# Sparse attention with a mixing network on one core: the last pair of heads of the first batch takes another way to its weights, its division and its low parts

## The chip, the cores and the metric

The kernel runs on one core of a Trainium2 chip (trn2). The metric is the time of one execution on the device in microseconds (us), the median of several executions. Lower is better. The engines are named as in the profile: PE is TensorE, DVE is VectorE, ACT is ScalarE, POOL is GpSimd, SP is SyncE, which here only issues DMAs.

## The reference, cut to what matters

There are 4 batches, 8 heads of width 64, and 576 tokens. Attention keeps the 32 largest scores of each row and gives them a softmax. Its output goes through two mixing networks.

```python
scores = scale * np.matmul(q, k.transpose(0, 1, 3, 2))          # [4, 8, 576, 576]
kth = np.partition(scores, -32, axis=-1)[..., -32:-31]
scores = np.where(scores >= kth, scores, -1e9)
attn = softmax(scores)                                           # sum + 1e-9 below the line
x = np.matmul(attn, v)                                           # then [batch, 576, 512]

theta = x @ w_theta                                              # network 1
y = einsum(w_tok_r, x * cos(theta)) + einsum(w_tok_i, x * sin(theta))
u = x + y
x = u + relu(u @ w_ch)

h = relu(x @ w_in)                                               # network 2
u, v = h[..., :512], h[..., 512:]
out = (u * (w_spatial @ layernorm(v) + b_spatial)) @ w_out
```

All of it is float32. PE multiplies rounded halves: each operand is split into a high part and a low part, and one product is three matmuls (high by high, high by low, low by high; `mm3`, L576 to L578).

## The kernel before, in words

**Attention.** A visit is one pair of heads of one batch, 16 visits in all, 4 per batch. A visit has 9 tiles: tiles 0 to 7 hold 128 rows of one head, tile 8 the last 64 rows of both. Two tiles make a group (G = 2), so there are 144 tiles and 72 groups, 18 groups per batch. For each group these steps follow one another:

- `scores`: PE multiplies (L449), ACT copies the result to the tile `x` (L453).
- `topk`: DVE folds each row into winners and losers (L468, L469), takes the best 8 of the losers as a guard (L472), and finds the 32 largest in four rounds of MAX8 (L478) and MATCH_REPLACE8 (L481). The threshold is the last value of `mx`. Two small ACT operations (L489, L490) and one on DVE (L491) make the numbers of the tile `cf` from it.
- `weigh`: ACT computes the sign of x minus the threshold into `sg` (L500) and the exponential of `x` in place (L501). POOL multiplies the two (L89, four pieces a group, since the helper `Pieces` cuts every POOL operation to at most 300 columns). What is below the threshold comes out negative.
- `transpose`: PE turns the result (L511), ACT copies it with a Relu, which makes the negatives zero (L512).
- `values`: PE multiplies by v (L533), with a column of ones that gives the row sums; ACT copies the result to `xr`. `normalise` divides: two small DVE operations (L564, L565), then a multiplication on POOL into `xn` (L89). The last visit of the first batch (visit 3) is normalised in four parts, as its tiles come.

**The networks.** The class `Front` prepares network 1 of a batch when its attention is done: it transposes `xn` (L689), splits it into high (`zah`) and low parts (`zal`, `last`), multiplies by w_theta, and takes sines and cosines on ACT, for which ACT loads another table and then loads the one of the exponential again. `rotate` then makes the operands of the token mixing: `zah`, `zal` with the cosine and `zbh`, `zbl` with the sine. The function `middle` runs the rest: 72 token-mixing products per batch accumulate in `ps_m`, DVE adds each result to the tile F (`F<-ps_m,F`), and so on through both networks. `last` is the last product. While one batch is in the networks, the next one is in attention: PE has the products between the matmuls of attention, and DVE has the top-k.

**What sets the order.** The program writes groups of attention, and after each half group lets the network's generator (`advance`) run until a quota is used up. A scheduler then orders each engine's instructions by its own model of time and by priorities: attention's steps have `AHEAD`, the front of the first batch has `FRONT` (higher), operations by `upool`, `udve`, `uact` have `URGENT`. Each engine then works through its list in that order, and waits at the first instruction whose inputs are not there. Beside this runs `conv`, which splits the weights (L163 to L170 and L211, tiles `w_raw` and `w_f`) and stores the parts by DMA.

```python
self.turns = [upool, udve] if b == B - 1 else [upool, upool]                    # who makes low parts
pool.tensor_tensor(sg, x, sg, op=OP.mult)                                       # weigh
pool.tensor_tensor(xn[:, i], xr[:, i, :, 0:D], rs[:, i, :, None]..., op=OP.mult)  # normalise
```

Of the kernel before, what the change touches and what calls it, by code (L numbers as in the profile page):

```python
# [10 lines left out]
F32 = mybir.dt.float32  # L11
F32R = mybir.dt.float32r
I32 = mybir.dt.int32
AF = mybir.ActivationFunctionType
# [10 lines left out]
def sparse_attention_then_moe_kernel(  # L25
# [310 lines left out]
    def run(exact):  # L336
# [96 lines left out]
        X, SG, MX, PT = {}, {}, {}, {}  # L433
        PER = NP * NT

        def scores(n):
            i, b, j, t = tiles[n]
            qs, ks, kl, dg = heads[i]
            ps = psum.tile([128, 2, 512], F32, name="ps_s")
            for c in range(2):  # L440
                o = ps[:, c, 0:HALF]
                m = slice(c * HALF, (c + 1) * HALF)
                if t < 8:
                    i, s = divmod(t, 2)
                    terms = [(qs[s][:, i * 128:(i + 1) * 128], k) for k in (ks[s], kl[s])]
                else:
                    terms = [(dg[s], k) for s in range(2) for k in (ks[s], kl[s])]
                for a, (q, k) in enumerate(terms):
                    pe.matmul(o, q, k[:, m], start=a == 0, stop=a == len(terms) - 1)  # L449
            if n % G == 0:  # L450
                X[n // G] = att.tile([128, G, S], F32, name="x", bufs=3)
            x = X[n // G][:, n % G]
            act.activation(x.rearrange("p (c n) -> p c n", c=2), ps[:, :, 0:HALF], AF.Copy)  # L453

        def topk(g):

            x = X[g]
            mx = att.tile([128, G, 32], F32, name="mx")
            mm = att.tile([128, G, S], F32, name="mm", bufs=1)
            if exact:  # L460
                src, mr = ([t[:, i] for i in range(G)] for t in (x, mm))
            else:


                z = att.tile([128, G, QUARTER + 16], F32, name="z", bufs=1)
                for t, lo, mid, hi, win in ((x, 0, HALF, S, mm), (mm, 0, QUARTER, HALF, z)):
                    a, b = t[:, :, lo:mid], t[:, :, mid:hi]
                    dve.tensor_tensor(win[:, :, 0:mid], a, b, op=OP.max)  # L468
                    dve.tensor_tensor(mm[:, :, mid:hi], a, b, op=OP.min)  # L469
                for k, losers in enumerate((slice(LOSERS, S), slice(QUARTER, LOSERS))):  # L470
                    for i in range(G):
                        dve.max(out=z[:, i, QUARTER + 8 * k:QUARTER + 8 * k + 8], in_=mm[:, i, losers])  # L472
                src = [z[:, i] for i in range(G)]
                mr = [mm[:, i, 0:QUARTER + 16] for i in range(G)]
            for r in range(4):
                top = [mx[:, i, 8 * r:8 * r + 8] for i in range(G)]
                for i in range(G):
                    last = dve.max(out=top[i], in_=src[i])  # L478
                if r < 3:
                    for i in range(G):  # L480
                        dve.match_replace(out=mr[i], in_to_replace=top[i], in_values=src[i], imm_value=NEG)  # L481
                    src = mr
            kth = mx[:, :, 31]
            if not exact:
                dve.tensor_tensor(flags[:, g], z[:, :, QUARTER + 7::8], mx[:, :, 31:32].to_broadcast([128, G, 2]),
                                  op=OP.is_gt)

            cf = att.tile([128, G, 3], F32, name="cf", bufs=3)
            act.activation(cf[:, :, 0], mx[:, :, 0], AF.Copy, scale=-0.125)  # L489
            act.activation(cf[:, :, 1], kth, AF.Abs, scale=ULP)  # L490
            dve.scalar_tensor_tensor(cf[:, :, 2], cf[:, :, 1], 1e-37, kth, op0=OP.max, op1=OP.subtract)  # L491
            MX[g] = cf
            GATE[g] = last.ins

        def weigh(n):
            x, cf = X[n // G][:, n % G], MX[n // G][:, n % G]
            if n % G == 0:
                SG[n // G] = att.tile([128, G, S], F32, name="sg", bufs=2)
            sg = SG[n // G][:, n % G]
            act.activation(sg, x, AF.Sign, bias=cf[:, 2:3])  # L500
            act.activation(x, x, AF.Exp, bias=cf[:, 0:1], scale=0.125)  # L501
            pool.tensor_tensor(sg, x, sg, op=OP.mult)
# [55 lines left out]
        def normalise(b, j, lo, hi):  # L558
            if lo == 0:
# [3 lines left out]
            rs = tmp.tile([128, 5, 2], F32, name="rs")  # L563
            dve.tensor_scalar(rs[:, i], xr[:, i, :, D], 1e-9, None, op0=OP.add)  # L564
            dve.reciprocal(rs[:, i], rs[:, i])  # L565
            pool.tensor_tensor(xn[:, i], xr[:, i, :, 0:D], rs[:, i, :, None].to_broadcast([128, hi - lo, 2, D]),
                               op=OP.mult)
            if hi == 5:
                if j == NP - 1:
                    WHOLE.add(b)  # L570
                pool.tensor_tensor(xn[64:128, 4], xr[0:64, 4, :, 0:D],
                                   rs[0:64, 4, :, None].to_broadcast([64, 2, D]), op=OP.mult)


# [86 lines left out]
        class Front:  # L661


            def __init__(self, b):
# [3 lines left out]
                self.za = [z[:, 0:2048].rearrange("p (k d) -> p k d", k=4) for z in zpair("a")]  # L668
                self.zb = None
                self.xh, self.xl = (z.rearrange("p k (c n) -> p k c n", c=4) for z in self.za)  # L670
                self.turns = [upool, udve] if b == B - 1 else [upool, upool]

            def z(self, k, d):
                return tuple(z[:, k, d] for z in self.za) if k < 4 else tuple(z[:, k - 4, d] for z in self.zb)
# [425 lines left out]
```

## Time and profile before

| what | value |
|---|---|
| median of 3 runs | 979.75 us (978.85 to 980.02) |
| profiled execution, its own time | 980.12 us |
| its span in the profile | 978.2 us |
| PE busy | 852.8 us (87%) |
| DVE busy | 822.4 us (84%) |
| ACT busy | 636.1 us (65%) |
| POOL busy | 597.0 us (61%) |

The span is the stretch from the first to the last instruction that the profiler recorded. The time of the execution is 1.9 us longer. All stretches below are counted from the start of the span. Top-k group 17, the last of the first batch, ends near 214 us, the last top-k group of all near 796 us; after that only the networks are left.

### The profile page before, as it was taken

To read this page: it belongs to the slowest core of one execution; us is meant where nothing else is said; L and a number is where in the kernel's file an instruction comes from. 1 tells how busy PE (TensorE), PEld (TensorE's weight loads), DVE (VectorE), ACT (ScalarE), POOL (GpSimd) and SP (SyncE) were. 2 spreads that over 40 slices of the span, in tenths; PEclk is the share of its full clock that TensorE was granted. 3 is DMA by queue.
4 is the path that set the end of the run, shared out by engine and by line. 5 is a ranking of instruction groups with operands and counts; after the bars stand their busy time and mean duration, and the time that the engine had idled before them with its cause. 6 is when DMAs were issued, how large, how long until landed. Compare 5 with 4: busy or idle time off the path is not lost.

```text
span 978.2 us, 18058 instructions
## 1 busy us (share of the span) xinstructions
PE 852.8 (87%) x5802; PEld 784.8 (80%) x5802; DVE 822.4 (84%) x2698; ACT 636.1 (65%) x1315; POOL 597.0 (61%) x749
## 2 busy tenths in 40 slices
PE   3748576679679999999999999899989999999997
PEld 2636455567569889897999998788889998889987
DVE  6999999999998998999899998999998971463552
ACT  5566677679777668877966778677956764350121
POOL 1798767576884867686576656775675464330030
PEclk9975666779679999999999999999999999999999
DMA  7797666555825743645352745372623545451221
GB/s 219 212 296 234 209 221 176 167 148 157 273 93 173 252 141 116 194 161 140 117 164 54 250 144 162 143 204 101 170 116 91 214 180 192 170 187 48 103 86 53
DMA packets 79395, 159.78 MB, mean 163 GB/s; under 512 B 36143, under 2 KB 40239, under 8 KB 71866
## 3 DMA queue, kind: packets, MB, share of 16 engines
q1 hardware_dynamic: 79290, 158.53, 51.5%
q8 instruction: 48, 0.79, 0.3%
q14 instruction: 57, 0.47, 0.1%
HBM read 108.63 MB, written 23.32 MB: 135 GB/s over the span
## 4 chain that ended last, share of the span: by engine, by line
PE 43%; DVE 28%; ACT 9%; DMA 8%; POOL 7%; issue 4%; SPq 2%; POOLq 0%; ACTq 0%; DVEq 0%
PE ps_m L578 9%; PE ps_m L576 9%; PE ps_m L577 9%; PE ps_v L533 6%; DVE mm L469 4%; DVE mx L478 4%; DVE mm L481 4%; PE ps_s L449 4%; PE ps_t L511 3%; DVE z L472 3%; DVE mm L468 3%; POOL sg L89 2%; DMA q<-hi 2%; POOL zbl L89 2%; ACT sg L500 1%
## 5 line engine op out<-in xcount | busy, mean ns | idle before, releaser
L89 POOL TENSOR_TENSOR sg<-x,sg 128x288 f32<-128x288 f32 x288 | 238.4, 857 | 135.0 <-ACT x L501 85.0
L533 PE MATMUL ps_v<-vc,ptb 128*128 128x65 f32 (+1 forms) x1280 | 179.2, 278 | 4.4 <-ACT ptb L512 4.4
L511 PE MATMUL ps_t<-ident,sg 128*128 128x128 f32 x648 | 137.4, 307 | 50.4 <-POOL sg L89 35.1
L533 PEld LDWEIGHTS ps_v<-vc,ptb 128*128 128x128 f32 (+1 forms) x1280 | 170.4, 202 | 13.2 <-ACT ptb L512 6.8
L511 PEld LDWEIGHTS ps_t<-ident,sg 128*128 128x128 f32 x648 | 96.0, 168 | 65.4 <-POOL sg L89 47.2
L500 ACT ACTIVATE sg<-x,cf 128x576 f32<-128x576 f32 x144 | 103.9, 769 | 54.1 <-DVE cf L491 50.4
L478 DVE MAX8 mx<-mm 128x8 f32<-128x160 f32 x432 | 120.2, 318 | 0.0
L512 ACT ACTIVATE ptb<-ps_t 128x640 f32<-128x640 f32 (+1 forms) x144 | 92.5, 642 | 31.7 <-PE ps_t L511 30.1
L449 PE MATMUL ps_s<-k,q 128*128 128x288 f32 x256 | 90.5, 365 | 23.5 <-ACT x L453 14.1
L501 ACT ACTIVATE x<-x,cf 128x576 f32<-128x576 f32 x144 | 108.3, 767 | 0.0
L453 ACT ACTIVATE x<-ps_s 128x576 f32<-128x576 f32 x144 | 92.3, 641 | 18.7 <-PE ps_s L449 15.4
L576 PE MATMUL ps_m<-w_t,zah 128*128 128x288 f32 (+2 forms) x272 | 97.7, 359 | 5.7 <-POOL zah L592 2.8
L578 PE MATMUL ps_m<-w_t,zal 128*128 128x288 f32 (+2 forms) x272 | 96.9, 357 | 0.5 <-POOL zal L89 0.5
L577 PE MATMUL ps_m<-w_t,zah 128*128 128x288 f32 (+2 forms) x272 | 95.7, 352 | 0.0
L472 DVE MAX8 z<-mm 128x8 f32<-128x312 f32 (+1 forms) x288 | 89.5, 372 | 2.0
L576 PE MATMUL ps_m<-w_t,zbh 128*128 128x288 f32 x288 | 85.3, 301 | 3.9 <-DVE F L592 2.1
L578 PE MATMUL ps_m<-w_t,zbl 128*128 128x288 f32 x288 | 84.9, 303 | 3.1 <-POOL zbl L89 3.1
L481 DVE MATCH_REPLACE8 mm<-mx,mm 128x160 f32<-128x160 f32 x288 | 87.7, 314 | 0.0
L577 PE MATMUL ps_m<-w_t,zbh 128*128 128x288 f32 x288 | 85.3, 300 | 0.0
L449 PE MATMUL ps_s<-kl,q 128*128 128x288 f32 x256 | 81.5, 329 | 0.0
L449 PEld LDWEIGHTS ps_s<-k,q 128*128 128x128 f32 x256 | 56.3, 220 | 29.9 <-ACT x L453 20.8
L89 POOL TENSOR_TENSOR raw<-raw,hi 128x288 fp32r<-128x288 f32 x60 | 55.7, 947 | 37.4 <-ACT hi L393 22.6
(167 smaller groups left out, 2438.8 us busy)
## 6 DMA issues: line engine op xcount, KB each, us to landing
k<-hi SPq DMA_DIRECT2D x60, 144.0 KB, 2.5
kl<-raw SPq DMA_DIRECT2D x60, 144.0 KB, 2.9
vc<-in_v_dram SPq DMA_DIRECT2D x48, 128.0 KB, 3.0
w_t<-d_trh SPq DMA_DIRECT2D x4, 1152.0 KB
w_t<-d_trl SPq DMA_DIRECT2D x4, 1152.0 KB
out_dram<-t SPq DMA_DIRECT2D x32, 144.0 KB, 2.5
raw<-in_q_dram SPq DMA_DIRECT2D x15, 288.0 KB, 3.2
q<-hi SPq DMA_DIRECT2D x30, 144.0 KB, 4.8
```

Source lines behind the costliest of these rows:

```text
L89: nc.gpsimd.tensor_tensor(out[:, lo:hi], a[:, lo:hi], b[:, lo:hi], op=op)
L449: pe.matmul(o, q, k[:, m], start=a == 0, stop=a == len(terms) - 1)
L472: dve.max(out=z[:, i, QUARTER + 8 * k:QUARTER + 8 * k + 8], in_=mm[:, i, losers])
L478: last = dve.max(out=top[i], in_=src[i])
L481: dve.match_replace(out=mr[i], in_to_replace=top[i], in_values=src[i], imm_value=NEG)
L500: act.activation(sg, x, AF.Sign, bias=cf[:, 2:3])
L501: act.activation(x, x, AF.Exp, bias=cf[:, 0:1], scale=0.125)
L511: pe.transpose(pt[:, c, :], x[:, lo:lo + 128], ident)
L533: pe.matmul(o, pt[:, c, q], chunks[:, c, slot], start=alone and c == 0, stop=not alone and i == 1 and c == 3)
L576: pe.matmul(out, ah, bh, start=first, stop=False)
L577: pe.matmul(out, ah, bl, start=False, stop=False)
L578: pe.matmul(out, al, bh, start=False, stop=last)
```

## The change

Three things change, all for the first batch, the first two for its last visit:

1. For group 17 (`QUICK`; tiles 7 and 8 of visit 3) ACT computes the exponentials right behind the first round of MAX8, when the largest value is known, into `sg` and not in place. When the threshold is known, DVE makes the mask and multiplies in one instruction per tile, x >= threshold times the exponential. The group has no Sign on ACT and no multiplication on POOL. Its `cf` is still made, and read by nobody.
2. `normalise` multiplies on DVE for visit 3.
3. In `Front` of the first batch DVE makes the low parts of every second tile (`zal` for token tiles 1 and 3, `last`, and `zbl` for two of the four column blocks), POOL the others.

```diff
+        QUICK = PER // G - 1
@@ topk, in the loop over the four rounds
+                if r == 0 and g == QUICK:
+                    most = att.tile([128, G], F32, name="most", bufs=1)
+                    act.activation(most, mx[:, :, 0], AF.Copy, scale=-0.125)
+                    SG[g] = att.tile([128, G, S], F32, name="sg", bufs=2)
+                    for i in range(G):
+                        act.activation(SG[g][:, i], x[:, i], AF.Exp, bias=most[:, i:i + 1], scale=0.125)
@@ topk, at the end
+            if g == QUICK:
+                with tc.high_priority(offset=FRONT):
+                    for i in range(G):
+                        e = SG[g][:, i]
+                        dve.scalar_tensor_tensor(e, x[:, i], mx[:, i, 31:32], e, op0=OP.is_ge, op1=OP.mult)
+                return
@@ weigh
+            if n // G == QUICK:
+                return
@@ normalise
-            pool.tensor_tensor(xn[:, i], ...
+            engine = dve if b == 0 and j == NP - 1 else pool
+            engine.tensor_tensor(xn[:, i], ...
-                pool.tensor_tensor(xn[64:128, 4], ...
+                engine.tensor_tensor(xn[64:128, 4], ...
@@ Front.__init__
-                self.turns = [upool, udve] if b == B - 1 else [upool, upool]
+                self.turns = [upool, udve] if b in (0, B - 1) else [upool, upool]
```

The scheduler makes a new order from this, and not only around group 17: the lists of PE, DVE, ACT, POOL and SP differ from there to the end of attention. Three places follow; the line numbers of the changed kernel are higher, by 2 in the first round of `topk` and by up to 17 further down (L592 is L609 there, L500 is L516, L501 is L517).

The first place is DVE at the end of top-k group 17. `sg<-x,mx,sg` is the new mask, `mm<-x` the first fold of group 18, `rs<-xr` the normalisation of visit 3. Before:

```order
L478 MAX mx<-mm 128x8 x2
L564 TENSOR_SCALAR rs<-xr 128x2
L163 TENSOR_SCALAR w_f<-w_raw 128x512
L468 TENSOR_TENSOR mm<-x 128x2x288
L469 TENSOR_TENSOR mm<-x 128x2x288
L565 RECIPROCAL rs<-rs 128x2
L485 TENSOR_TENSOR flags<-z,mx 128x4
```

And after the change:

```order
L480 MAX mx<-mm 128x8 x2
L163 TENSOR_SCALAR w_f<-w_raw 128x512
L506 SCALAR_TENSOR_TENSOR sg<-x,mx,sg 128x576
L470 TENSOR_TENSOR mm<-x 128x2x288
L506 SCALAR_TENSOR_TENSOR sg<-x,mx,sg 128x576
L471 TENSOR_TENSOR mm<-x 128x2x288
L609 COPY F<-ps_m 128x128
```

The two masks stand between the last maximum of group 17 and the folds of group 18, and the small operations of `normalise` have moved up into group 17.

The second place is ACT around the sines of the first batch, `zbl<-zbl,upright` and `zbh<-zbh`, behind their table load. `w_f<-w_f` is the splitting of weights by `conv`; `cf<-mx` at L490 (L498) belongs to the group whose top-k has just ended. Before:

```order
L592 ACTIVATE zbl<-zbh 128x512
L211 ACTIVATE w_f<-w_f 128x576
L592 ACT_TABLE_LOAD
L592 ACTIVATE zbl<-zbl,upright 128x4x256 x2
L592 ACTIVATE zbh<-zbh 128x4x256 x2
L490 ACTIVATE cf<-mx 128x2
L453 ACTIVATE x<-ps_s 128x576
```

And after the change:

```order
L609 ACTIVATE zbl<-zbh 128x512
L211 ACTIVATE w_f<-w_f 128x576
L528 ACTIVATE ptb<-ps_t 128x512
L609 ACT_TABLE_LOAD
L609 ACTIVATE zbl<-zbl,upright 128x4x256 x2
L609 ACTIVATE zbh<-zbh 128x4x256 x2
L455 ACTIVATE x<-ps_s 128x576
```

The `w_f<-w_f 128x576` shown is the third with 576 columns before the change and the first after it, and the sines stand two top-k groups earlier: among the work of group 20 where they were among that of group 22.

The third place is SP. `w_t<-d_tih` and `w_t<-d_til` are the two parts of the weights w_tok_i, which can be fetched when the product with w_theta has freed its buffers; `k` and `kl` are the keys of visit 5, `w_f` and `w_raw` belong to `conv`. Before:

```order
L284 DMA w_t<-d_tih 128x2304
L284 DMA w_t<-d_til 128x2304
L219 DMA d_s5h<-w_f 64x576
L199 DMA w_f<-in_moe_w_spatial_dram 128x576
L219 DMA d_s5h<-w_f 64x576
```

And after the change:

```order
L284 DMA w_t<-d_tih 128x2304
L284 DMA w_t<-d_til 128x2304
L199 DMA w_f<-in_moe_w_spatial_dram 128x576
L224 DMA d_iuh<-w_f 128x512
L408 DMA k_2646<-hi 64x576 x2
L225 DMA d_iul<-w_f 128x512
L408 DMA k_2647<-hi 64x576
```

The two fetches now stand ahead of all eight copies of the keys of visit 5; before, they stood behind them.

## Rows read from the trace of the kernel before

**Rows 1.** Page, part 1: the span, then busy time of an engine

```profile
span 978.2 us, 18058 instructions
```

**Rows 2.** Stretches: busy us (count) of PE, PEld, DVE, ACT, POOL; PE clock, DMA share, GB/s

```profile
235.80:311.10 75.30, 60.33 (x373) 54.35 (x371) 69.77 (x195) 58.26 (x110) 55.56 (x66) 0.82 0.60 189
311.10:786.90 475.80, 454.11 (x3404) 427.84 (x3404) 448.51 (x1586) 354.17 (x750) 321.46 (x403) 0.99 0.50 153
786.90:978.00 191.10, 182.31 (x1255) 170.68 (x1253) 81.96 (x229) 63.11 (x135) 55.43 (x71) 1.00 0.35 130
```

**Rows 3.** DVE in order of time: start, us, [idle before]: groups 20 and 25 begin, first fold

```profile
235.81 0.74 DVE L468 TENSOR_TENSOR mm<-x 128x576 f32<-128x576 f32 x1
...
311.12 0.74 DVE L468 TENSOR_TENSOR mm<-x 128x576 f32<-128x576 f32 x1
311.79 0.74 DVE L469 TENSOR_TENSOR mm<-x 128x576 f32<-128x576 f32 x1
```

**Rows 4.** ACT in order of time, up to the first sines of the first batch

```profile
258.17 0.69 ACT L211 ACTIVATE w_f<-w_f 128x576 fp32r<-128x576 f32 x1 [2.12 <-DMA w_f<-in_moe_w_spatial_dram]
258.87 1.28 ACT L592 ACT_TABLE_LOAD   x1
260.17 2.19 ACT L592 ACTIVATE zbl<-zbl,upright 128x1024 f32<-128x1024 f32 x2
```

**Rows 5.** Who DVE waited for from 235.8 to 311.1 us: total, times, longest

```profile
DVE zbl L592 <- ACT zbl L592: 2.1, 1, 2.1
DVE w_f L163 <- ACT w_f L211: 1.7, 1, 1.7
DVE F L592 <- PE ps_m L578: 0.7, 1, 0.7
```

**Rows 6.** DVE groups from 235.8 to 311.1 us: count, busy us, mean ns, idle before

```profile
L469 DVE TENSOR_TENSOR mm<-x 128x576 f32<-128x576 f32 x5 | 5.6, 1117 | 0.0
...
L468 DVE TENSOR_TENSOR mm<-x 128x576 f32<-128x576 f32 x5 | 3.9, 782 | 0.0
...
L592 DVE COPY F<-ps_m 128x128 f32<-128x128 f32 x2 | 0.6, 281 | 0.0
L592 DVE COPY F<-ps_m 128x256 f32<-128x256 f32 x1 | 0.4, 414 | 0.0
```

**Rows 7.** DVE in order of time: three low parts in a row, a fold beside POOL

```profile
271.43 1.88 DVE L592 TENSOR_TENSOR zal<-zbl,zah 128x512 fp32r<-128x512 f32 x3
...
279.16 1.28 DVE L469 TENSOR_TENSOR mm<-x 128x576 f32<-128x576 f32 x1
```

**Rows 8.** POOL in order of time beside that fold

```profile
273.45 6.38 POOL L89 TENSOR_TENSOR zbl<-xn,zbh 128x256 fp32r<-128x256 f32 x8 [2.57 <-ACT zbh L592]
279.79 4.13 POOL L89 TENSOR_TENSOR sg<-x,sg 128x288 f32<-128x288 f32 x4
```

**Rows 9.** DVE in order of time: one top-k group from its first maximum to its end

```profile
231.37 0.54 DVE L478 MAX8 mx<-z 128x8 f32<-128x160 f32 x2
...
234.94 0.75 DVE L163 TENSOR_SCALAR w_f<-w_raw 128x512 int32<-128x512 int32 x1
```

**Rows 10.** ACT in order of time: two Signs of one group, one exponential

```profile
228.26 1.45 ACT L500 ACTIVATE sg<-x,cf 128x576 f32<-128x576 f32 x2
...
231.14 0.78 ACT L501 ACTIVATE x<-x,cf 128x576 f32<-128x576 f32 x1
```

**Rows 11.** PE in order of time: token mixing; scores that waited for ACT

```profile
272.08 0.30 PE L576 MATMUL ps_m<-w_t,zah 128*128 128x288 f32 x1
272.21 0.29 PE L577 MATMUL ps_m<-w_t,zah 128*128 128x288 f32 x1
...
290.76 0.61 PE L449 MATMUL ps_s<-k,q 128*128 128x288 f32 x1 [3.64 <-ACT x L453]
```

**Rows 12.** DVE in order of time: top-k groups 41 and 42 begin

```profile
472.79 0.76 DVE L468 TENSOR_TENSOR mm<-x 128x576 f32<-128x576 f32 x1 [1.23 <-ACT x L453]
...
493.00 0.75 DVE L468 TENSOR_TENSOR mm<-x 128x576 f32<-128x576 f32 x1
```

More of the change, by code (lines that the diff above doesn't have):

```diff
@@ L565, in normalise @@
             dve.reciprocal(rs[:, i], rs[:, i])
-            pool.tensor_tensor(xn[:, i], xr[:, i, :, 0:D], rs[:, i, :, None].to_broadcast([128, hi - lo, 2, D]),
+            engine = dve if b == 0 and j == NP - 1 else pool
+            engine.tensor_tensor(xn[:, i], xr[:, i, :, 0:D], rs[:, i, :, None].to_broadcast([128, hi - lo, 2, D]),
                                op=OP.mult)
@@ L570, in normalise @@
                     WHOLE.add(b)
-                pool.tensor_tensor(xn[64:128, 4], xr[0:64, 4, :, 0:D],
+                engine.tensor_tensor(xn[64:128, 4], xr[0:64, 4, :, 0:D],
                                    rs[0:64, 4, :, None].to_broadcast([64, 2, D]), op=OP.mult)
```

## The prediction

> **What bounds the kernel now.** I read the span first [rows 1]. The profiled execution took 980.12 us, 1.9 us more than its span and 0.37 us more than the median of the runs, 979.75 us. I make the sum against 980.1 and take 0.4 off at the end.
>
> Then I cut the span into stretches [rows 2]. Behind 786.9 us, when the last top-k group begins, DVE is busy 82 of 191 us and PE 182: PE sets the end there. From 311.1 to 786.9 us both are nearly full: PE 454.1 of 475.8 us (95%), DVE 448.5 (94%). The stretch that the change works on is 235.8 to 311.1 us, which is top-k groups 20 to 24 together with the front of the first batch [rows 3]. Here DVE is busy 69.8 of 75.3 us (93%), PE only 60.3 (80%), POOL 55.6 (74%). So for 75 us PE has 15.0 us to spare and DVE 5.5, and for the next 475 us neither has much. This is the view to keep in mind: work that PE could do before 311 us would be worth something later, and what DVE is given costs at once.
>
> Why does PE starve? The front is a long chain from the last `xn` to the first token-mixing product, through a table load on ACT, and DVE works through it between the rounds of top-k. Just ahead of the sines ACT stands still for 2.12 us on a weight that arrives late, then loads its table for 1.28 us [rows 4]. DVE waits 2.1 us for those sines, 1.7 us for ACT's splitting of a weight and 0.7 us for PE [rows 5]. PE waits in its turn, 3.64 us in one place for ACT to take away scores [rows 11].
>
> **The change part by part.**
>
> *What DVE gets.* Fifteen instructions. By starts in a row, a fold of 128x576 takes 0.67 us [rows 3] and a low part of 128x512 takes (1.88 - 0.07) / 3 = 0.60 us [rows 7]; 0.07 us is the overlap of 0.74 us of duration with the next start [rows 3]. The two masks are as wide as a fold: 2 x 0.67 = 1.3 us. The two wide `zbl` blocks: 2 x 0.60 = 1.2 us. Eight pieces of 128x128 or less (three `xn` and one of 64 rows, two `zal`, two narrow `zbl`) I price by the copy of that size, 0.281 us less 0.07, so 8 x 0.21 = 1.7 us; three of 128x256 (one `xn`, two `last`) by 0.414 less 0.07: 3 x 0.34 = 1.0 us [rows 6]. Together **+5.3 us** (5.2 before rounding the parts). The copies read PSUM, so the true price may be a little lower.
>
> *What POOL loses.* Nineteen pieces: four `sg`, five `xn`, two `zal`, two `last`, six `zbl`. The wide ones take 6.38 / 8 = 0.80 us each [rows 8]. POOL is not full, but its pieces hold up DVE: beside POOL's `zbl` and `sg` a fold took 1.28 us [rows 7, 8] that takes 0.74 us alone [rows 3], 0.54 us more. Averaged over two kinds of fold, 1.117 and 0.782 us [rows 6], the lengthening is (0.38 + 0.04) / 2 = 0.21 us for each DVE instruction with two tiles as inputs. The fifteen new ones can be held up too: 15 x 0.21 = 3.2 us. What nineteen POOL pieces cost DVE can't be read from one row; at 0.54 us each it is at most 10.3 us, and a third of that, 3.4 us, would fit the mean. I let the two cancel: **0**, with -10 and +8 (15 x 0.54) as the ends.
>
> *A wait that is added.* The masks wait for ACT's exponentials, and behind them on DVE stands all of group 18's top-k. From the first maximum to the end of a group DVE needs 3.6 us [rows 9]. In this time ACT has, in its new order, two operations of two columns, an exponential, the two Signs of group 16, and the second exponential: 0.78 + 1.45 + 0.78 [rows 10] and about 0.4 for the small ones, 3.4 us. It just fits if ACT comes to it at once. I take **+0.5 us**, between 0 and 2.
>
> *What moves ahead.* In the new order the sines stand among group 20's work, not group 22's, and only the first of the weight splits with 576 columns is still ahead of them, not three. So the 2.12 us wait of ACT [rows 4] falls behind the sines, and DVE's 2.1 us wait for them should shrink. Of DVE's 5.5 us idle I count these 2.1 us and half of the remaining 3.4: **-3.8 us**, between 0 and -5.5. What may be late next: DVE reaches `zbl<-xn,zbl` sooner as well, so part of the wait can stay.
>
> The two fetches of w_tok_i move ahead too, in front of eight copies of keys on SP. They are 2 x 1.18 MB; at 189 GB/s [rows 2] that is 12 us of transfer. It costs nothing as long as these keys are needed later by about as much: group 22, the first that uses them, now comes behind the whole front and not before it. Without that cover it is up to 12 us for the scores of that group.
>
> *What PE wins.* I counted token-mixing products ahead of each group's first transpose in both orders. At groups 21, 22 and 23 the new order is 61, 55 and 63 products ahead; at 24, 25 and 26 only 11, 17 and 8. The lead melts because the quotas hand out the work per group: at groups 56, 57, 59, 70 and 71 both orders have exactly the same count. A product takes 0.13 us, from the starts at 272.08 and 272.21 us [rows 11]. What is left when PE becomes full is some 14 products, **-1.8 us**; the ends are 0 and 61 x 0.13 = -8 us.
>
> Sum: 5.3 + 0 + 0.5 - 3.8 - 1.8 = +0.2 us. 980.1 + 0.2 - 0.4 gives **979.9 us**: gain and cost cancel within what I can see.
>
> A rule speaks against the change. The Trainium skill's page "Perfetto Trace Analysis", section "Identifying the Most-Contended Engine", says to find the engine with the highest occupancy and to relieve that one first. Of the engines that it judges by occupancy that is DVE here, and the change loads it. By that rule the added work would come out in full, the first rival below.
>
> **The rivals.**
>
> *DVE decides (slower).* DVE is 93% busy in the stretch and 94% after it [rows 2], and the change gives it 5.3 us and takes nothing away. If the lead of PE is worth nothing, because the orders agree again by group 26, and ACT's chain still makes DVE wait its 2 us, then 5.3 + 0.5 - 1.7 = +4 us: 984 us. For it: DVE's share, and the quotas. Against it: the POOL pieces that vanish, and PE's 95% after 311 us, which says that DVE alone is not the limit. It decides where group 25 starts later than 311.1 + 2 us in the new trace.
>
> *PE decides (faster).* If the 8 us of products at groups 21 to 23 really run in PE's idle 15 us, and PE is the limit for the next 475 us, then top-k goes faster right behind the front, and POOL's absence gives DVE something too: 5.3 + 0.5 - 3.8 - 8 = -6, so 974 us. For it: PE idle 15.0 of 75.3 us. Against it: the counts at groups 24 to 26, and that PE starved because of DVE's work, which is no smaller.
>
> *The rest of the order decides (either sign).* The scheduler shuffled batches 1 to 3 too. The front of the second batch comes a group later: its sine products, all in group 41 before, are all in 42 now. That group took 20.2 us [rows 12]. In the new order PE is 35 products behind at groups 41 and 46, and 56 at group 50, and makes it up by 56. 35 x 0.13 = 4.6 us of PE work is pushed into groups that are already full: up to +5 us; other places may give as much.
>
> *The change does not do what it says.* If the exponentials are late on ACT, the masks make DVE stand, and tiles 7 and 8 are no sooner at PE than by Sign and POOL. Then the front stays where it was in time though not in the order, and the cost is 5.3 + 2 = +7 us, 987 us.
>
> **How the numbers follow.** What a measurement of this kernel can tell from no change is about 0.2%, or 2 us. Forecast (979.9 us, its own range 976 to 983.5): 0.53, of which 0.31 lies within 2 us, 0.14 below and 0.08 above. PE decides: 0.17, faster. DVE decides: 0.14, slower. The rest of the order: 0.13, of which 0.07 faster and 0.06 slower. The change fails: 0.03, slower. Faster 0.38, same 0.31, slower 0.31. The range reaches to both rivals with their unknowns: 972 to 987 us.
>
> **What would show it.** Right: ACT's sines of the first batch near 243 us instead of 260 [rows 4], with no 2 us of idle on ACT or DVE beside them; the first long run of token mixing on PE 15 us or more sooner; DVE busy about 5 us more and POOL some 14 us less (19 pieces of at most 0.80 us); group 25 starting within 2 us of 311, and the same distance in time kept to group 70. Wrong: idle time on DVE ahead of the masks named after ACT's exponential; scores of group 22 waiting for a DMA; group 25 early by 5 us or more, which would mean that I took the lead of PE or the load of POOL too small; or a difference that arises only behind group 40, which would be the new order and not the edits themselves.

## The result: 989.6 us where 979.9 was predicted, and the profile after

| | before | after |
|---|---|---|
| median of the runs | 979.75 us (976.24 to 980.79, 5 runs) | 989.57 us (985.62 to 995.01, 5 runs) |
| ratio after / before | | 1.0109, 95% interval 1.0067 to 1.0152 |
| profiled execution, its span | 980.12, 978.2 | 991.46, 989.6 |
| busy PE, DVE, ACT, POOL | 852.8, 822.4, 636.1, 597.0 | 860.4, 829.7, 633.7, 592.4 |

Slower by 1.1%, and 2.6 us beyond the upper end of the range. Part 1 of the page of the changed kernel:

```profile
span 989.6 us, 18046 instructions
...
PE 860.4 (87%) x5802; PEld 785.8 (79%) x5802; DVE 829.7 (84%) x2713; ACT 633.7 (64%) x1314; POOL 592.4 (60%) x730
```

The spans differ by 11.4 us; the medians differ by 9.8, since the profiled execution was 1.9 us above its median. Where do the 11.4 us arise? The changed kernel in stretches (columns as in [rows 2]): groups 20 to 24, 25 to 35, 36 to 70, and the tail from group 71 on.

```profile
241.30:315.80 74.50, 61.43 (x430) 56.07 (x430) 67.91 (x201) 58.07 (x109) 51.61 (x54) 0.95 0.65 205
315.80:435.50 119.70, 108.32 (x736) 99.62 (x735) 109.27 (x387) 82.08 (x187) 83.30 (x102) 0.91 0.47 145
435.50:800.40 364.90, 347.95 (x2611) 327.32 (x2610) 348.55 (x1197) 270.37 (x564) 243.63 (x303) 1.00 0.47 147
800.40:989.60 189.20, 180.09 (x1238) 168.53 (x1236) 81.72 (x228) 62.05 (x132) 54.25 (x70) 1.00 0.35 131
```

The kernel before in groups 25 to 35, same view:

```profile
311.10:422.70 111.60, 106.88 (x802) 100.83 (x802) 105.96 (x393) 82.92 (x190) 80.77 (x99) 1.00 0.58 171
```

Group 25 starts at 315.8 instead of 311.1 us: +4.7. Groups 25 to 35 take 119.7 instead of 111.6: **+8.1**, the largest item. Groups 36 to 70 take 0.7 more (364.9, before 364.2), the tail 2.1 less (189.2; [rows 2] has 191.1, 191.3 with its last 0.2). In groups 25 to 35 PE is idle for 11.4 us, before for 4.7, and its clock is 0.91 on the mean, before 1.00.

These eleven groups can be cut in two, groups 25 to 28 and 29 to 35. After the change, then before:

```profile
315.80:356.20 40.40, 35.61 (x226) 33.32 (x224) 37.34 (x132) 27.73 (x63) 31.83 (x39) 0.83 0.50 160
356.20:435.50 79.30, 72.71 (x512) 66.30 (x511) 71.93 (x257) 54.35 (x124) 51.47 (x65) 0.96 0.46 137
```

```profile
311.10:350.40 39.30, 36.25 (x283) 35.34 (x283) 38.96 (x135) 27.59 (x64) 30.33 (x38) 1.00 0.56 181
350.40:422.70 72.30, 70.63 (x520) 65.49 (x520) 67.00 (x260) 55.34 (x128) 50.43 (x63) 1.00 0.59 166
```

Of the 8.1 us, 1.1 arise by group 29 and 7.0 behind it. Of PE's 6.7 us more of idle time, 1.7 arise by group 29 and 4.9 behind it.

I also split DVE's time by its rows: idle time; lengthening, which is what an instruction takes above the tenth percentile of those of its operation, names and shapes in both kernels; and the rest, its own work. Own work and lengthening are good to some 0.5 us.

| groups | own work before, after | lengthening | idle |
|---|---|---|---|
| 17 to 24 | 82.9, 90.3 | 20.7, 15.8 | 6.3, 8.4 |
| 25 to 35 | 86.7, 87.1 | 19.3, 22.1 | 5.6, 10.4 |
| of these, 25 to 28 | 30.8, 31.1 | 8.1, 6.1 | 0.3, 3.1 |
| of these, 29 to 35 | 55.6, 56.0 | 11.4, 15.9 | 5.3, 7.4 |
| 36 to 70 | 290.3, 293.0 | 52.2, 55.6 | 21.6, 16.4 |

**The front did come sooner.** ACT in order of time, to the first sines:

```profile
244.60 0.68 ACT L211 ACTIVATE w_f<-w_f 128x576 fp32r<-128x576 f32 x1 [1.22 <-DMA w_f<-in_moe_w_spatial_dram]
...
245.78 1.28 ACT L609 ACT_TABLE_LOAD   x1
247.08 2.19 ACT L609 ACTIVATE zbl<-zbl,upright 128x1024 f32<-128x1024 f32 x2
```

The sines start 13.1 us earlier than in [rows 4]. The waits beside them moved along: ACT still waits for a weight, and DVE for the sines (who DVE waited for, 241.3 to 315.8 us; before in [rows 5]):

```profile
DVE xn L609 <- ACT t L609: 2.4, 1, 2.4
DVE zbl L609 <- ACT zbl L609: 1.9, 1, 1.9
```

By group 25 PE has issued 1225 matmuls, before 1146; the last of the eight sums of the token mixing comes 14.8 us earlier. DVE in order of time in the changed kernel: a new wait, the masks, the start of group 20, that sum, the start of group 25.

```profile
211.26 0.34 DVE L580 TENSOR_SCALAR rs<-xr 128x2 f32<-128x2 f32 x1 [1.66 <-ACT xr L562]
...
215.45 0.81 DVE L506 SCALAR_TENSOR_TENSOR sg<-x,mx,sg 128x576 f32<-128x576 f32 x1
...
216.84 1.35 DVE L506 SCALAR_TENSOR_TENSOR sg<-x,mx,sg 128x576 f32<-128x576 f32 x1
...
241.25 0.74 DVE L470 TENSOR_TENSOR mm<-x 128x576 f32<-128x576 f32 x1
...
313.56 0.44 DVE L609 TENSOR_TENSOR F<-ps_m,F 128x288 f32<-128x288 f32 x1
...
315.83 0.75 DVE L470 TENSOR_TENSOR mm<-x 128x576 f32<-128x576 f32 x1
```

The same sum before:

```profile
328.34 0.45 DVE L592 TENSOR_TENSOR F<-ps_m,F 128x288 f32<-128x288 f32 x1
```

**Where the lead went.** The next product needs the sums split into `ph` and `pl`. These tiles lie in the buffers (tags "ph" and "pl") in which `conv` splits the weights (`w_raw` and `w_f` in the function `split_rest`). As long as the splitting still uses these buffers, `ph` and `pl` can't be written; below this is called the lock. POOL in the changed kernel:

```profile
312.93 1.41 POOL L89 TENSOR_TENSOR w_f<-w_f 128x256 fp32r<-128x256 f32 x2
319.21 2.00 POOL L89 TENSOR_TENSOR xn<-xr,rs 128x128 f32<-128x128 f32 x4 [4.87 <-DVE rs L581]
322.19 4.15 POOL L89 TENSOR_TENSOR sg<-x,sg 128x288 f32<-128x288 f32 x4 [0.98 <-POOL xn L89]
326.30 2.05 POOL L89 TENSOR_TENSOR pl<-F,ph 128x288 fp32r<-128x288 f32 x2
```

And before:

```profile
309.63 1.44 POOL L89 TENSOR_TENSOR w_f<-w_f 128x256 fp32r<-128x256 f32 x2 [2.27 <-DVE mx L478]
314.66 3.87 POOL L89 TENSOR_TENSOR pl<-F,ph 128x288 fp32r<-128x288 f32 x5 [3.59 <-DMA vx<-in_v_dram]
...
331.72 1.32 POOL L89 TENSOR_TENSOR pl<-F,ph 128x288 fp32r<-128x288 f32 x1
```

The weights were finished at 311.1 us before the change and at 314.3 after it: they did not move up with the front. Before, five sums were waiting then; after, all eight, and `pl` also stands behind `xn` and `sg` in POOL's list. So a token mixing that ends 14.8 us sooner gives its last `pl` no sooner (331.7 us before, 332.1 after). What PE makes of it, in order of time:

```profile
315.35 0.62 PE L593 MATMUL ps_m<-ph,w_t 128*128 128x288 f32 x3
318.39 0.83 PE L527 MATMUL ps_t<-ident,sg 128*128 128x128 f32 x4 [2.42 <-ACT ptb L528]
...
327.43 0.61 PE L594 MATMUL ps_m<-pl,w_t 128*128 128x288 f32 x1 [1.56 <-POOL pl L89]
```

From 311 to 327 us in stretches of 4 (columns as above):

```profile
311.00:315.00 4.00, 2.53 (x19) 2.16 (x19) 4.00 (x21) 3.37 (x8) 3.34 (x4) 1.00 1.02 381
315.00:319.00 4.00, 1.58 (x11) 1.15 (x10) 3.93 (x13) 4.00 (x13) 0.00 (x0) 0.97 1.11 293
319.00:323.00 4.00, 3.80 (x17) 3.29 (x15) 4.00 (x25) 3.72 (x9) 2.73 (x6) 0.50 1.02 409
323.00:327.00 4.00, 2.87 (x14) 2.47 (x13) 3.93 (x7) 0.98 (x3) 4.00 (x4) 0.50 0.76 233
```

PE starts no product that needs `pl` for 12 us, is busy 4.1 of 8 us from 311 to 319, and then has half the clock (1.2 GHz) to 332 us. Its lead over the kernel before, in matmuls issued, goes from 79 at the start of group 25 to 37 at group 26 and 21 at group 29. Top-k lost little in this time: by group 29 it is 5.8 us late, after 4.7 at group 25.

### The profile page after: what moved, and what is told of

Its sections match the earlier page's. It is cut to its first block, busy times and chain, and to the rows that moved or that the text cites. A ratio compares the mean times of both kernels' runs of the same rounds, so it can differ in the third digit from the quotient of the medians.

```text
span 989.6 us, 18046 instructions
## 1 busy us (share of the span) xinstructions
PE 860.4 (87%) x5802; PEld 785.8 (79%) x5802; DVE 829.7 (84%) x2713; ACT 633.7 (64%) x1314; POOL 592.4 (60%) x730
## 4 chain that ended last, share of the span: by engine, by line
PE 31%; DVE 29%; ACT 5%; POOL 3%; issue 2%; DMA 2%; SPq 0%; DVEq 0%; ACTq 0%; POOLq 0%
PE ps_m L595 7%; PE ps_m L593 7%; PE ps_m L594 7%; DVE mx L480 5%; DVE mm L489 5%; DVE mm L471 4%; DVE z L474 3%; PE ps_v L549 3%; DVE mm L470 3%; PE ps_s L451 2%; PE ps_t L527 2%; DVE F L609 2%; DVE flags L493 2%; DVE z L470 1%; DVE st L609 1%
## 5 line engine op out<-in xcount | busy, mean ns | idle before, releaser
L516 ACT ACTIVATE sg<-x,cf 128x576 f32<-128x576 f32 x142 | 102.5, 769 | 49.6 <-DVE cf L499 49.6
L517 ACT ACTIVATE x<-x,cf 128x576 f32<-128x576 f32 x142 | 106.2, 768 | 0.1
L470 DVE TENSOR_TENSOR mm<-x 128x576 f32<-128x576 f32 x72 | 71.9, 998 | 15.7 <-ACT x L455 14.4
L89 POOL TENSOR_TENSOR raw<-raw,hi 128x288 fp32r<-128x288 f32 x60 | 61.0, 1037 | 32.3 <-ACT cf L497 14.4
```

What stands on the lines that cost most here:

```text
L89: nc.gpsimd.tensor_tensor(out[:, lo:hi], a[:, lo:hi], b[:, lo:hi], op=op)
```

## The experiments

Letters: A, load and waits at the front make the loss, and the parts of the change add; B, the loss is made in groups 28 to 35, where DVE and POOL fall against each other, and depends on the order and not on the parts; C, the late order (behind group 36) makes it. Later D, the buffers of the weight splitting lock the gain; E, they don't matter. In the small kernels and in the one with the overlapping pieces the letters mean what stands beside them in brackets.

All runs in one table. "25" is the start of group 25 against before, "25 to 35" what these groups take, then PE's idle time in them, and the matmuls that start behind group 71, all from the profiled execution.

| kernel | median us | ratio (95%) | 25 | 25 to 35 | PE idle | behind 71 |
|---|---|---|---|---|---|---|
| before | 979.75 | | | 111.6 | 4.7 | 1253 |
| after | 989.57 | 1.0109 (1.0067 to 1.0152) | +4.7 | 119.7 | 11.4 | 1236 |
| no_masks | 986.53 | 1.0073 (1.0050 to 1.0097) | -0.9 | 122.5 | 10.1 | 1253 |
| no_norm | 988.65 | 1.0103 (1.0079 to 1.0127) | +4.5 | 114.8 | 4.6 | 1297 |
| no_low | 986.58 | 1.0068 (1.0042 to 1.0094) | +1.7 | 119.2 | 8.5 | 1238 |
| late_order | 979.40 | 1.0008 (0.9992 to 1.0024) | +0.8 | 111.5 | 4.7 | 1238 |
| after_split16 | 980.84 | 1.0017 (0.9993 to 1.0040) | +7.9 | 111.7 | 3.0 | 1263 |
| after_split13 | 981.14 | 1.0017 (0.9998 to 1.0035) | +5.8 | 111.7 | 4.0 | 1207 |
| before_split16 | 988.34 | 1.0089 (1.0062 to 1.0115) | +2.3 | 111.0 | 3.6 | 1319 |
| before_split10 | 989.90 | 1.0101 (1.0076 to 1.0127) | +1.4 | 121.3 | 6.5 | 1253 |
| after_gap | 990.25 | 1.0100 (1.0080 to 1.0121) | +3.4 | 121.3 | 12.7 | 1238 |
| after_split12 | 987.01 | 1.0070 (1.0048 to 1.0092) | +6.5 | 113.3 | 3.9 | 1253 |
| after_split14 | 983.09 | 1.0034 (1.0013 to 1.0055) | +11.8 | 109.0 | 3.6 | 1265 |
| after_split17 | 987.30 | 1.0098 (1.0068 to 1.0128) | +1.6 | 116.3 | 2.8 | 1253 |
| no_low_split17 | 990.15 | 1.0093 (1.0062 to 1.0124) | +3.8 | 120.4 | 7.2 | 1223 |

**One part taken back at a time, and the late order alone.** The edits to the changed kernel (one each), and to the kernel before (`late_order`: eight writes of a constant behind group 40, which give the order behind group 41 that the changed kernel has):

```diff
-        QUICK = PER // G - 1
+        QUICK = -1
...
-            engine = dve if b == 0 and j == NP - 1 else pool
+            engine = pool
...
-                self.turns = [upool, udve] if b in (0, B - 1) else [upool, upool]
+                self.turns = [upool, udve] if b == B - 1 else [upool, upool]
...
+            if g == 40 and not exact:
+                for _ in range(8):
+                    dve.memset(xr[64:128, 4], 1.0)
```

> The change without its first part: group 17 is weighed as before (Sign, exponential in place, POOL multiplies); normalising and half of the low parts stay on DVE. In its order the front stands in group 21 and everything behind group 45 is as before the change. Theory A (load: what is lost comes from the work given to DVE at the front, about 5 us of the 10, and from waits there): 2 to 3 us less than the changed kernel, so +7 us against the kernel before; group 25 starts 2 to 3 us late. Theory B (lottery: most is lost in groups 28 to 35, where DVE and POOL fall against each other in a new order): the loss between groups 28 and 35 depends on this order and not on the parts, so it may be gone or larger: between -2 and +10 us, with group 25 at +2 to +3. Theory C (the order behind group 36 decides): back to +0 to +3 us.

> The change without its second part: visit 3 is normalised on POOL again. Front in group 21; the order behind group 41 is a third one, in which PE is up to 12 us of products behind the order before. Theory A: 1 to 2 us less than the changed kernel, +8 us. Theory B: no rule, -2 to +10 us; group 25 at +3 to +4. Theory C: slower than the changed kernel, +10 to +15 us, the loss arising behind group 41.

> The change without its third part: POOL makes all low parts of the first batch. Front in group 21; the order behind group 39 is that of the changed kernel to the last product. Theory A: 2 to 3 us less than the changed kernel, +7 us, group 25 at +2. Theory B: no rule, -2 to +10 us; whatever is lost arises by group 36, and from there the distance to the kernel before stays as it does in the changed kernel (within 2 us). Theory C: as the changed kernel, +10 us, arising behind group 39.

> The kernel before, with eight writes of a constant (64 rows of ones that are there already) on DVE at group 40. They cost about 1 us and make the planner put the front of the second batch one group later; from group 41 on the products stand in the order of the changed kernel, and up to group 38 everything is as before. Theory A and theory B: within 2 us of the kernel before. Theory C: +8 to +10 us, like the changed kernel.

C falls for the changed kernel: with its late order the time is that of before. `no_norm`, which has another late order, did come out as C had it: 10 us slower, with its last 8 us lost in the tail, where 44 matmuls more were left at group 71. Whether the parts add can't be told: without any one of them the kernel is still 0.7 to 1.0% slower than before, with all three 1.1%, and these intervals overlap. The times of `no_masks` and `no_low`, some 7 us above before, are the ones that A named; the place is not. `no_masks` is at group 25 as early as before and loses 10.9 us in the next eleven groups, 7.2 of them in groups 29 to 35. The changed kernel loses 7.0 there and `no_low` 5.2, so B has the place right for these three; `no_norm` loses nothing there. So A explains what there is at group 25, and the rest arises later, in one place or another.

**The weights split sooner.** The edit, to the changed kernel and, as a control, to the one before (with 16, 13, 10):

```diff
-    SPLIT = 21
+    SPLIT = 16
```

> The changed kernel, with the splitting of the weights handed out whole at group 16 and not at group 21. Theory D (the gain of the front is locked behind the weights): in the changed kernel the token mixing ends 15 us sooner (eighth sum of F at 313.6 us, before 328.3), but ph and pl of the next product lie in the buffers of the splitting, whose last part POOL finishes at 313.6; ph starts at 314.8, pl at 326.3, PE falls idle and to half clock in 312 to 332, and DVE waits. With the splitting done earlier, ph and pl should start before 300 us, PE should keep 2.4 GHz from 311 to 340, DVE's idle in groups 25 to 29 should fall from 4.4 us to about 1, and the time from 989.6 to 983 or less. Theory E (load and hold-ups on DVE alone; the wait for the buffers is slack): the same work only comes earlier, ahead of the front, the time stays at 987 to 992.

> As the last one, with the splitting handed out at group 13: pl stands in POOL's order at group 20, where it stood at 24. D: as with 16, 983 us or less. E: 987 to 992.

> The kernel before with the same move (group 16): its front is not earlier, its ph and pl come right behind the last weight at 310.7, with only half of the token mixing done by then. D: the buffers are not what it waits for, so within 3 us of 979.7. E: within 3 us as well; it is the control for what the move does by itself. Worse than that would be its late order, where PE is 5 to 12 us of products behind at groups 41 to 71.

> The kernel before with the splitting handed out at group 10: sines at group 21, pl at group 22 in POOL's order, the late order that of before. D: the front comes one group sooner and nothing is locked, so 974 to 980 us. E: within 3 us of 979.7.

Both changed kernels come down by 8 us or more, as D says, to 981 us. By the profile they are only 4.7 and 6.9 us sooner than the changed kernel at group 36, since group 25 starts 3.2 and 1.1 us later in them. POOL in `after_split13`:

```profile
288.23 4.26 POOL L89 TENSOR_TENSOR w_f<-w_f 128x256 fp32r<-128x256 f32 x4 [1.86 <-ACT w_f L211]
...
295.08 1.57 POOL L89 TENSOR_TENSOR pl<-F,ph 128x288 fp32r<-128x288 f32 x2 [2.59 <-DMA d_oul<-w_f]
...
318.50 0.93 POOL L89 TENSOR_TENSOR pl<-F,ph 128x288 fp32r<-128x288 f32 x1 [1.89 <-ACT ph L609]
```

The second row shows the lock: the first `pl` waits for the store of the last weight, `d_oul<-w_f`. Now this ends at 295 us, the last `pl` comes 1.9 us behind the last sum (316.56), and groups 25 to 35 take 111.7 us at full clock (stretch of `after_split13`):

```profile
316.90:428.60 111.70, 107.68 (x795) 99.81 (x795) 103.39 (x389) 83.78 (x188) 79.73 (x99) 1.00 0.56 172
```

In `after_split16` it is less clean. Its `ph` came at 298.6 and `pl` at 302.5 us, 2.5 us later than D allowed, DVE was idle for 3.3 us in groups 25 to 29, not 1, and PE still had 0.66 of its clock from 310 to 325 us; yet PE's idle time in groups 25 to 35 fell to 3.0 us and their time to 111.7. The gain doesn't lie where the lock stood: groups 25 to 28 take 42.6 us here, the changed kernel's take 40.4, and groups 29 to 35 take 69.1 instead of 79.3. In `after_split13` the two stretches take 38.4 and 73.3 us.

A kernel above speaks against D too. In `no_masks` the weights were finished at 302.9 us without any edit to the splitting, its `ph` started at 302.2, and its `pl` came 15 us sooner than in the changed kernel (POOL):

```profile
L89 POOL TENSOR_TENSOR pl<-F,ph x8: 792/802/811, 305.7 to 317.1; 128x288 fp32r<-128x288 f32 x8
```

The last sum of its token mixing came at 313.9 us, as in the changed kernel, and its last `pl` followed in 3.2 us. Yet its groups 25 to 35 take 122.5 us, more than the changed kernel's.

The controls missed both expectations: 9 and 10 us slower than before. `before_split16` finished its weights no sooner (310.7 us), so it shows nothing of an open buffer; it is as fast as before to group 71 and then has 66 matmuls more to do, as its expectation feared of its late order: its tail takes 201.5 us. `before_split10` loses 10 us between groups 30 and 36, where DVE is idle for 14.4 us (before 5.2). So moving the splitting is no gain by itself, and an order can lose 10 us in places that have nothing to do with the lock.

**Four more orders.** Group 12, 14 and 17 in the changed kernel, and 17 without part 3 (edits as above):

> The changed kernel with the weight splitting handed out whole at group 12. In its order PE is 3 to 9 us of products ahead of the kernel before at groups 25 to 60 and 3.6 us at group 71. D: groups 25 to 36 take no longer than before the change (111.6 us, in the changed kernel 119.7); with the lead kept, 972 to 980 us, better than both. E (any new order costs about the same): 986 to 992.

> The same with group 14; its late order is that of the kernel before (no lead at groups 57 to 71). D: groups 25 to 36 in 110 to 114 us, and 977 to 983 us. E: 986 to 992.

> The same with group 17; its late order has the front of each later batch a group or two later (sines in groups 43 and 63), and PE stands 10 to 19 us of products behind from group 39 to the end, 15.7 us at group 71. D: groups 25 to 36 in 110 to 114 us, but a tail longer by what PE has left, so 985 to 996 us, with the loss behind group 36. E: about 990 too, but with the loss at groups 25 to 36.

> The changed kernel without its third part (POOL makes all low parts, 8 DVE instructions fewer), splitting handed out at group 17; PE ahead by 3 to 10 us at groups 21 to 35, 4 us at group 71, the late order of after_split12. D: 970 to 979 us, the best of all. E: 984 to 990.

The late orders that these expectations name for 12, 14 and 17 were read wrongly. The traces have 1253, 1265 and 1253 matmuls behind group 71 (before 1253), so no lead and no debt, and the times that I derived from them fall out. What is left is D's statement on groups 25 to 35. PE's idle time in them is 3.9, 3.6 and 2.8 us, as D would have it; they take 113.3, 109.0 and 116.3 us, two of the three above D's figure, and all three below the changed kernel's 119.7. In groups 25 to 28 alone they take 37.0, 41.8 and 44.5 us (the changed kernel 40.4), so for two of the three the gain again lies in groups 29 to 35. `after_split14` in this stretch:

```profile
322.90:431.90 109.00, 105.43 (x788) 98.95 (x787) 102.39 (x389) 83.06 (x187) 80.29 (x99) 1.00 0.56 170
```

`no_low_split17` didn't escape the lock, since its `ph` starts at 312.7 and its `pl` here (POOL):

```profile
319.65 1.57 POOL L89 TENSOR_TENSOR pl<-F,ph 128x288 fp32r<-128x288 f32 x2 [5.48 <-DMA raw<-in_k_dram]
```

Its groups 25 to 35 take 120.4 us, like the changed kernel's. It was to be the best of all and is one of the slowest. None of these kernels beats the one before.

**A fold that stood for 5.42 us.** In group 34 of the changed kernel (DVE):

```profile
409.33 5.42 DVE L470 TENSOR_TENSOR mm<-x 128x576 f32<-128x576 f32 x1
414.67 1.27 DVE L471 TENSOR_TENSOR mm<-x 128x576 f32<-128x576 f32 x1
```

POOL beside it:

```profile
409.10 0.76 POOL L609 TENSOR_SCALAR t<-t,st 64x512 f32<-64x512 f32 x1
409.83 1.56 POOL L89 TENSOR_TENSOR sg<-x,sg 128x288 f32<-128x288 f32 x2
411.36 2.77 POOL L89 TENSOR_TENSOR zbl<-vt,zbh 128x256 fp32r<-128x256 f32 x4
414.21 2.31 POOL L89 TENSOR_TENSOR zbh<-t,zbh 64x256 fp32r<-64x256 f32 x2
```

It takes 0.74 us alone [rows 3], and here it ends 0.6 us behind POOL's row of seven pieces without a gap (411.36 + 2.77 = 414.13). These 4.7 us are as much as DVE's whole lengthening grew in groups 29 to 35 (4.5). `no_masks` and `no_low` have the same in the same place (4.66 and 5.44 us). Two small kernels and an edit asked what it is and what it costs.

```python
act.activation(go, ...)                                   # starts both
for k in range(n): pool.tensor_tensor(po_k, pa, pb, op=OP.mult)
for k in range(phase): dve.max(out=mx, in_=a[:, 0:160])
dve.tensor_tensor(fold, a, b, op=OP.max)
```

> A small kernel that computes none of the reference: 54 trials. In each, ACT starts POOL and DVE together; POOL runs 1, 2, 4 or 8 multiplications of 128x288 behind one another, DVE runs 0 to 5 maxima of 128x160 (so that it arrives at another point of POOL's run) and then one two-input fold of 128x576, alone 0.74 us. Further trials with 8 pieces: a write of one column, or of 64 columns, on POOL between the pieces; POOL's pieces with one input; DVE's instruction with one input (a scaling, a maximum). Theory B (a fold that arrives inside a run waits for the run to end): with 8 pieces the fold takes up to 8 x 0.7 = 5.6 us, in steps with its point of arrival, and with 1 piece at most 1.4; the one-input maximum stays as it is alone. Theory A (POOL holds a fold for one piece at most, and the 5.42 us had another cause): no fold takes over 1.5 us, whatever the length of the run.

> The small kernel once more, computing none of the reference, with POOL's pieces writing apart from one another (none depends on the one ahead), as in the large kernel, 1, 2, 4 or 8 of them, and six trials with 8 pieces of 128x256. B: without a gap between the pieces the fold waits for several of them, up to the end of the run: over 2 us with 4 pieces, over 4 with 8. Rival (a run's length doesn't matter, only the moment of arrival): no fold over 1.5 us here either, and the 5.42 us need something else, such as PE's or ACT's traffic beside it.

In neither did a fold take over 1.4 us: 1.38 at most in the first, where 0.08 us lay between the pieces, and 1.23 in the second, where none did. DVE, then POOL, in a trial of `micro_hold2` with eight pieces:

```profile
86.95 1.20 DVE L56 TENSOR_TENSOR fold<-a,b 128x576 f32<-128x576 f32 x1
```

```profile
86.00 6.54 POOL L47 TENSOR_TENSOR po<-pa,pb 128x288 f32<-128x288 f32 x8
```

So a run's length alone doesn't hold a fold in these kernels. The edit let the second piece of a low part in `norm_tiles` begin on the last column of the first, so that they depend on one another (changed kernel, first batch, tiles 2 to 4):

```diff
+                    for lo, hi in zip(cuts, cuts[1:]):
+                        lo = max(lo - 1, 0)
+                        upool.tensor_tensor(out[:, lo:hi], a[:, lo:hi], b[:, lo:hi], op=op)
```

> The changed kernel; for the first batch the second piece of each low part that norm_tiles(2, 3, 4) gives to POOL begins one column earlier, on the last column of the first piece. So the pieces depend on one another, which in the small kernel left 0.08 us between them and let a fold in after one piece. Nothing else is edited; up to group 33 the order differs in a few rows only. Theory B (the 4.7 us that group 34's fold lost in POOL's run of pieces are lost for good): no DVE instruction near 409 us over 3.5 us, group 36 starts 3 to 6 us sooner than in the changed kernel (435.5 us), and the time is 984 to 987. Theory D (what counts is that PE starves at 312 to 332 us behind the buffers of the weight splitting): the fold is short, and the time stays at 988 to 991, since DVE only waits elsewhere.

The fold still took 4.04 us, and another, near 335 us, 4.73; the time stayed where it was. What was to be removed wasn't, so this tells little; group 36 starts 13.1 us late here and 12.7 in the changed kernel, whichever fold stood. The held fold stays a rival to the lock: the four kernels with a fold held for over 4 us in groups 25 to 35 (the changed one, `no_masks`, `no_low`, `after_gap`) take 119.2 to 122.5 us there, and of the eleven others nine take 109.0 to 116.3.

## Why the prediction was wrong, step by step

*What DVE gets: +5.3.* Right in size. DVE's own work in groups 17 to 24 grew by 7.4 us, of which some 1.1 are three sums of the token mixing that now come ahead of group 25 (three times 0.45 less 0.07); that leaves some 6.3.

*What POOL's absence gives: 0 between -10 and +8.* In the bounds: lengthening fell by 4.9 us in these groups and rose by 6.2 behind them, +1.3 in all, so the 0 was near for the whole kernel. POOL's busy time fell by 4.6 us only, not 14, since its other pieces took longer.

*The masks' wait: +0.5.* Right: both masks run without a wait. But `normalise` moved up too, and its `rs` waits 1.66 us for ACT's `xr`, with top-k behind it. I had quoted that move and not priced it.

*Waits that go: -3.8.* Wrong in sign. DVE's idle time in groups 20 to 24, from which this was to come, rose from 5.5 to 6.6 us. The sines came 13 us sooner (247, not 243), and every wait of the chain came with them. What I had called possible, that "part of the wait can stay", was the rule.

*PE's lead: -1.8.* **The step that failed.** Everything behind group 25 was to gain 1.8 us; it cost 6.7 (8.1 in groups 25 to 35, 0.7 in 36 to 70, less 2.1 in the tail). The lead was there, 79 matmuls at group 25. I let it melt in the quotas, and asked of the front alone what is late next. Late next was the buffer of `ph` and `pl`, held by the weight splitting until 314.3 us, and then POOL's list. PE fell idle and to half its clock, and the lead was down to 21 matmuls at group 29.

That the lock took the lead is seen in the trace. That it made the 8.1 us is not shown. For it: where the splitting alone was moved, in five changed kernels, PE's idle time in groups 25 to 35 fell from 11.4 us to between 2.8 and 4.0, and the stretch by 3.4 to 10.7 us. Against it: only 1.1 of the 8.1 us arise by group 29 (DVE idle for 2.8 us more and lengthened by 2.0 less), and the other 7.0 behind 356 us, 24 us after PE had its clock back. DVE's rows there show 4.5 us more of lengthening, as much as the one held fold, and 2.1 more of idle time. `no_masks`, where the lock ended 11 us sooner, lost 10.9 us in these groups, and `before_split10` 9.7. No run undid the lock with the rest of the order held. So the cause of the 7.0 us stays open between the order, the held fold and a late effect of the lock.

*The rivals.* "DVE decides" had its condition met (group 25 more than 2 us late), and its price, +4, is near the 4.7 us that stand at group 25. That is in part luck: its terms were 5.3, 0.5 and -1.7, and the rows have 7.4 of own work, 4.9 less of lengthening and 2.1 more of idle time. It lacked the rest. By the rule that I quoted from the Trainium skill's page "Perfetto Trace Analysis", section "Identifying the Most-Contended Engine", the added work would come out in full; the trace agrees in part, since 4.9 of the 7.4 us came back beside POOL. "The rest of the order" was the right worry at the wrong place: not at groups 41 to 50, as `late_order` shows, but in groups 25 to 35, most of it from group 29 on. "PE decides" fell, since a lead of PE that top-k can't use is handed back by group 71: `after_split17` is 80 matmuls ahead at group 36 and has as many left at group 71 as the kernel before (1253).

*Range and chances.* I gave slower 0.31 and ended the range at +7. What no case held is that a new order by itself is worth up to 10 us (the rival named 5, and as much in other places): changed kernels in six orders took 980.8 to 989.6 us (mean 984.8; `after_gap`, not among them, 990.3), kernels without the change in four orders 979.4 to 989.9 (mean 984.3). The change's own price can't be told apart from this; change and order together lost 9.8 us.

## What to carry to other kernels

When a stage is pulled forward, look up who holds the buffers of the stage behind it. Here the shared tags held five of eight sums before the change already, and it was no loss, since PE had other work (busy for all of 307 to 323 us). Ask also where a lead is kept: PE ran ahead into the lock, and lost its lead and, here, its clock. Then look whether the time is lost where the lock stands; here it was 1.1 of 8.1 us, and `no_masks`, where the lock ended 11 us sooner, lost as much. And where a scheduler makes the order, time a change in several orders (move one harmless number) before crediting or blaming it: here the orders of one kernel lay 10 us apart.

## What the runs showed of the hardware that I had not expected

A 0.74 us fold beside POOL's pieces of 0.8 us took at most 1.38 us in the small kernels. A maximum with one input kept its 0.76 us there, while a scaling with one input, 0.46 us alone, took up to 1.03. In the large kernels, of 1331 folds in fifteen of them that began while POOL was running, 1321 took under 1.5 us. Eight took over 2 us, up to 5.44: they stood through three to seven of POOL's pieces, which themselves weren't lengthened, and got in at the end of the run. What sets these eight apart stays open. It is not the length of the run alone, since 189 folds began with eight pieces or more to come, the running one counted, and none of them took over 1.6 us.

The Trainium skill's page "SBUF — State Buffer", section "Who interferes with whom", says that a DVE instruction with two SBUF inputs contends with a GpSimd instruction that reads SBUF, and calls the port pair that they share an exclusive lock. If the later one waits for one instruction of the other, a fold would be held for one piece of 0.8 us at most, an estimate of 1.5 us for the whole. The small kernels agree with it, and so do the 1321 folds; the eight do not.
